# A SwiGLU block behind linear attention on one core: the first product of the last down projection is split by a second Strassen level too

## The chip, the core and the metric

The kernel runs on one core of a Trainium2 chip. TensorE (PE) multiplies matrices and writes to PSUM, VectorE (DVE) and ScalarE (ACT) take results out of PSUM and do elementwise work, GpSimd (POOL) does elementwise work between SBUF operands and issues some DMAs, and SyncE (SP) issues most DMAs. The metric is the device time of one execution in microseconds (us); the kernel before takes 757.95 us (median of three runs, 757.32 to 758.75).

## The reference

```python
xn = layernorm(x)                        # x: 2048 x 1024
s  = linear_attention(xn, wqkv) @ wo     # 32 heads of 32
g  = silu((silu(xn @ w_gate) * (xn @ w_up)) @ w_down)   # 1024 -> 3584 -> 1024
out = x + s * g
```

All inputs and the output are bf16. What the change touches is the last product, `(...) @ w_down`, for one half of the 2048 rows.

## The kernel before

The feed-forward part works in two passes of 1024 rows. In a pass, `h` holds the product of gate and up, transposed: `h[:, c, :]` is row chunk `c` (128 of the 3584 hidden columns) by 1024 tokens. The pass has 28 *units*, 14 pairs of a gate unit and an up unit, each for 256 hidden columns. A unit is one matrix product by Strassen (Winograd's form): `emit_a` issues four products of four matmuls of 512 columns, `emit_b` three more. They interleave on PE: the `a` part of unit i+1 stands ahead of the `b` part of unit i. So the `a` part of unit k starts when the `b` part of unit k-2 is done. `emit_c22` and `emit_evac` take a unit's results out of PSUM with ACT and DVE. `x_` and `y_` are PSUM banks of pool `pps` (4 banks), `zw` pairs of banks of pool `ppd` (2 pairs).

A unit's weights and their four Strassen sums were packed in DRAM earlier (`pk_g`, `pk_u`) and come back in one DMA of 1 MB into a slot of the ring `wgu` (8 slots, `w_slot`). `load_w_to(n)` issues the loads up to the n-th in the sequence `w_seq`; a load whose slot is still in use waits at the head of SP's queue, and everything behind it on SP waits too.

After the units of the last pass, `emit_down_m` computes the down projection of that pass by Strassen: seven products M1 to M7 over quadrants of `h` (A11, A12, A21, A22) and of `w_down`, in the order 1, 2, 7, 6, 5, 4, 3. A plain product is 56 matmuls of 512 columns (4 row tiles by 14 chunks, line L1400). M2 and M4 are split once more (`L2 = (2, 4)`, function `l2_M`): each becomes seven products of 14 matmuls of 256 columns (L1433), with partial results copied between PSUM banks by ACT (L1449, L1455) and added by DVE (L1388). `KA` and `KB` are fp32 buffers in SBUF that hold M1 and the running sums of M1, M7 and M6.

The second level needs sums of quadrants on both sides:

- Of the weights, *staging* does it during the units of the last pass. `l2_load` takes a ring slot and issues the loads of two of the seven chunk pairs (four DMAs of 128 KB, L1109; two for the last pair), `l2_sums` does four subtractions on POOL (L1122) and stores the seven blocks to DRAM with a DMA from POOL (L1123, 896 KB). There are four such steps for a product, so eight for M2 and M4, one in every third unit (`i % 3`).
- Of `h`, `l2_lhs` does four sums on POOL per chunk pair (L1139 to L1142), into two `kept` tiles that the first pass left over (`x_spare`). For M2 it runs during the units, for the last chunk pair and for M4 afterwards.

At the end `fin` multiplies by `s` (L1176), adds `x` (L1177) and stores (L1178).

Of the kernel before, what the change touches and what calls it, by code (L numbers as in the profile page):

```python
# [21 lines left out]
def kernel(  # L22
# [168 lines left out]
    L2 = (2, 4)  # L191
    L2_ORDER = (1, 5, 2, 6, 7, 4, 3)
# [759 lines left out]
    with ExitStack() as p3:  # L952
# [4 lines left out]
        p3a = ExitStack()  # L957
        pps = p3a.enter_context(tc.tile_pool(name="p3ps", bufs=4, space=PSUM, reuse_waits="tile"))
        ppd = p3a.enter_context(tc.tile_pool(name="p3pd", bufs=2, space=PSUM, reuse_waits="tile"))
# [62 lines left out]
        def emit_evac(key, h, tail=None):  # L1022
            p, kind, fg = key
            x_, zw, s2, s3, _, *c = grp.pop(key)
            rc = rc_of(key)
            if kind == "g":
                cf = m4.tile([P, 2, TB], FP32, name="cg", tag="m4")
                d12 = cf[:]
            else:
                c = c[0]  # L1030
                d12 = c[:, 0:2, :]
                sg = sg_tiles.pop((p, fg))
                nc.vector.scalar_tensor_tensor(out=h[:, 2 * fg, 0:TB], in0=x_[:], scalar=rc, in1=sg[:, 0, :],
                                               op0=ALU.mult, op1=ALU.mult)
            nc.vector.scalar_tensor_tensor(out=d12, in0=zw[:], scalar=rc,  # L1035
                                           in1=s2[:, None, :].to_broadcast([P, 2, TB]), op0=ALU.mult, op1=ALU.add)
            if kind == "g":
                sg = m4.tile([P, 4, TB], BF16, name="sg", tag="m4")
                sg_tiles[(p, fg)] = sg
                nc.scalar.activation(out=sg[:, 3, :], in_=s3[:], func=ACT.Silu)  # L1040
                nc.scalar.activation(out=sg[:, 0, :], in_=x_[:], func=ACT.Silu, scale=rc)
                nc.scalar.activation(out=sg[:, 1:3, :], in_=cf[:], func=ACT.Silu)  # L1042
            else:
                if tail is not None:
                    tail()
                hv = h[:, 2 * fg:2 * fg + 2, :].rearrange("p a b -> p (a b)")
                nc.vector.tensor_tensor(out=hv[:, TB:4 * TB], in0=c[:].rearrange("p a b -> p (a b)"),
                                        in1=sg[:, 1:4, :].rearrange("p a b -> p (a b)"), op=ALU.mult)
# [51 lines left out]
        def l2_load():  # L1100
# [5 lines left out]
            for j in js:  # L1106
                for k, b0, b1 in ((0, 0, 7), (1, 2, 6)):
# [4 lines left out]
        def l2_sums():  # L1112
# [5 lines left out]
            def b(i):  # L1118
                r = v[:, i, 0:n_, :]
                return r.bitcast(F16) if i in (1, 3, 4, 5) or M >= 4 else r  # L1120
            for o_, a_, b_ in ((1, 7, 0), (3, 6, 1), (4, 6, 7), (5, 2, 3)):
                nc.gpsimd.tensor_tensor(out=b(o_), in0=b(a_), in1=b(b_), op=ALU.subtract)  # L1122
            nc.gpsimd.dma_start(out=l2_drams[M][:, :, js.start:js.stop, :], in_=v[:, 0:7, 0:n_, :])  # L1123

        x_spare = []

        def l2_bufs():
            v = [x[:].rearrange("p a b -> p (a b)").bitcast(F16)[:, 0:2 * NQ * 2 * P].rearrange(
                "p (s j r n) -> p s j r n", s=2, j=NQ, r=2) for x in x_spare]
# [6 lines left out]
        def l2_lhs(A, j, eng):  # L1136
            a11, a12, a21, a22 = l2_quad(A, j)
            s1, s2, s3, s4 = [v[:, j] for v in l2_bufs()]
# [226 lines left out]
        def emit_down_m(p, h, base):  # L1365
# [8 lines left out]
            def load(M, q=None):  # L1374

                load_w_to(base + max(i for i, key in enumerate(seq) if key[2][0] == M and q in (None, key[2][1])) + 1 + NPK)
# [30 lines left out]
            p3a.close()  # L1407
            ppm = p3.enter_context(tc.tile_pool(name="p3m8", bufs=2 * TPB, space=PSUM, reuse_waits="tile"))

            def banks(n=TPB):  # L1410
                return [ppm.tile([P, CW], FP32, name="dm", tag="m")[:] for _ in range(n)]
# [10 lines left out]
            def l2_p(M, i, r, A, bk):  # L1422
# [6 lines left out]
                for j in range(NQ):  # L1429
                    q = l2_quad(A, j)  # L1430
                    sb = [v[:, j] for v in l2_bufs()]
# [4 lines left out]
            def l2_M(M, A, K, done, fill, in_place):  # L1436
# [3 lines left out]

                def xw(r):
                    return bk[2 * r]

                def zy(r):
                    return bk[2 * r + 1]
                for i, r in ((1, 0), (5, 0), (1, 1), (5, 1)):
                    l2_p(M, i, r, A, bk)
                for r in range(2):
                    nc.scalar.copy(out=zy(r)[:, hi], in_=xw(r)[:, lo])  # L1449
                load(M, 0)  # L1450
                c = [[k2([P, CW], FP32, "l2c")[:] for _ in range(2)] for r in range(2)]
                for r in range(2):
                    l2_p(M, 2, r, A, bk)
                    l2_p(M, 6, r, A, bk)
                    nc.scalar.copy(out=zy(r)[:, lo], in_=zy(r)[:, hi])  # L1455
                    tt(K[2 * r][:, hi] if in_place else c[r][0][:, hi], zy(r)[:, hi], K[2 * r][:, hi])
                load(M, 1)
                for r in range(2):
                    l2_p(M, 7, r, A, bk)
                for r in range(2):  # L1460
                    tt(c[r][1][:, hi], zy(r)[:, lo], K[2 * r + 1][:, hi])
                    tt(c[r][1][:, hi], xw(r)[:, hi], c[r][1][:, hi])
                    if not in_place:
                        tt(c[r][0][:, lo], xw(r)[:, lo], K[2 * r][:, lo])
# [4 lines left out]
                for r in range(2):  # L1469
                    tt(c[r][1][:, lo], zy(r)[:, lo], K[2 * r + 1][:, lo])  # L1470
                    done(2 * r + 1, c[r][1])
                    l2_p(M, 3, r, A, bk)
                    if in_place:
                        tt(c[r][0], xw(r), K[2 * r])
                    else:
                        tt(c[r][0][:, hi], xw(r)[:, hi], c[r][0][:, hi])
                    done(2 * r, c[r][0])
                load(M, 3)

# [7 lines left out]
            load_w_to(base + NPK)  # L1487
            bk = banks()
            E = [bk[2], bk[3], bk[0], bk[1]]
            KA = kept("kA")  # L1490
            for t0 in (0, 2):
                for k in range(NFG):
                    for t in (t0, t0 + 1):
                        mm(1, t, k, E[t], True)
                for t in (t0, t0 + 1):
                    nc.scalar.copy(out=KA[t], in_=E[t])
            load(1)
            for k in range(NFG):
                tt(S3(k), A11[:, k], A21[:, k], ALU.subtract)
            sums(S1, A21, A22, ALU.add)  # L1500

# [10 lines left out]
            l2_M(2, quads(h, 1, 0), KA, done2, fill7, False)  # L1512
# [8 lines left out]
            for j in range(NQ):  # L1521
                l2_lhs(quads(h, 1, 1), j, nc.gpsimd)
# [29 lines left out]
            l2_M(4, quads(h, 1, 1), KB, done4, fill3, True)  # L1552
# [18 lines left out]
        for pi, p in enumerate(passes):  # L1571
# [71 lines left out]
            l2_steps = [] if first else list(l2_q)  # L1643
# [6 lines left out]
            for i in range(n):  # L1650
                if first:
                    load_w_to(base + i + (na0 if i < n - 7 else 8 if i > n - 6 else 7))
                else:
                    load_w_to(base + i + (6 if i < 3 * len(l2_steps) else 8))
# [34 lines left out]
                if not first:  # L1689
                    if i % 3 == 0 and l2_q:  # L1690
                        l2_load()
                    if i % 3 == 1 and l2_live:
                        l2_sums()
                    if i % 4 == 0 and i >= 4:
                        l2_lhs(quads(h, 1, 0), i // 4 - 1, nc.gpsimd)
                    if i == n - 1:
                        l2_lhs(quads(h, 1, 0), NQ - 1, nc.gpsimd)
# [3 lines left out]
            if last_pass:  # L1701
                emit_down_m(p, h, base)
# [35 lines left out]
```

## Time and profile before

| What | Value |
|---|---|
| median of the runs | 757.95 us |
| profiled execution, its own time | 757.71 us |
| span of its trace | 755.9 us |
| PE busy | 746.6 us, 99% |
| DVE, ACT, POOL busy | 573.5, 379.5, 361.1 us |
| TensorE clock granted | 1.00 |
| DMA, mean over the span | 242 GB/s |
| last pass: first `a` part to the last `b` part | 497.66 to 667.36 us |
| down projection of the last pass on PE | 667.36 to 751.31 us |

Busy time tells little of PE here: matmuls overlap, so a group's busy time is longer than its share of the span, and the distance between the starts of two groups is the better measure. The chain of waits is read from its end: each piece is what the next one waited for. In the timelines of SP and POOL a DMA's row is its issue, not its transfer.

### The profile page before, as it was taken

What the parts mean: (1) busy time and instruction counts of PE and PEld (TensorE: products, weight loads), DVE (VectorE), ACT (ScalarE), POOL (GpSimd) and SP (SyncE); (2) the same over time, 40 slices, a digit from 0 to 9 for tenths busy, and PEclk for the clock granted to TensorE, in tenths of its full rate; (3) what the DMA queues carried; (4) which work ended last, traced back from release to release, by engine and by line L of the source; (5) the groups of instructions that cost most, each with busy time, mean ns of one, the idle gap of its engine ahead of it and who ended that gap; (6) DMA issues with size and microseconds to landing.
All of it is one profiled execution on the core that took longest, in us unless ns stands there. A gap on an engine that the chain in (4) does not pass through costs nothing.

```text
span 755.9 us, 10887 instructions
## 1 busy us (share of the span) xinstructions
PE 746.6 (99%) x3815; PEld 356.8 (47%) x3815; DVE 573.5 (76%) x1036; ACT 379.5 (50%) x537; POOL 361.1 (48%) x444
## 2 busy tenths in 40 slices
PE   8999999999999999999999999999999999999997
PEld 3544444454544444444444444444444444446464
DVE  6687787886796788888889765369686777784965
ACT  5677776898956565666659301142322223212023
POOL 2444799999540276858675000115344433113900
PEclk9999999999999999999999999999999999999999
DMA  9967799979779667878899236498867567748452
GB/s 318 304 146 137 234 329 301 306 157 270 217 180 304 232 215 280 315 275 308 279 331 391 92 120 242 131 373 296 307 248 275 194 241 251 266 156 257 165 169 82
DMA packets 123896, 183.19 MB, mean 242 GB/s; under 512 B 35936, under 2 KB 99424, under 8 KB 114112
## 3 DMA queue, kind: packets, MB, share of 16 engines
q1 hardware_dynamic: 116496, 151.41, 62.3%
q0 software_dynamic: 5904, 28.58, 9.9%
q10 hardware_dynamic: 1440, 2.49, 1.0%
q8 instruction: 30, 0.49, 0.3%
q14 instruction: 26, 0.21, 0.1%
HBM read 118.10 MB, written 57.02 MB: 232 GB/s over the span
## 4 chain that ended last, share of the span: by engine, by line
PE 96%; DVE 2%; issue 1%; DMA 0%; ACT 0%; DVEq 0%; ACTq 0%
PE zw L966 25%; PE kv_ps L554 15%; PE xb L966 12%; PE q_ps L183 7%; PE dm L1400 7%; PE dzw L1204 6%; PE yb L966 6%; PE dx L1204 3%; PE s_ps L774 3%; PE fx L816 3%; PE dm L1433 3%; PE dy L1204 2%; PE nd L743 1%; PE kvz L576 1%; DVE g L1176 1%
## 5 line engine op out<-in xcount | busy, mean ns | idle before, releaser
L966 PEld LDWEIGHTS <-w_sb 128*128 128x128 f16 (+1 forms) x1568 | 152.2, 98 | 183.2 <-issue 0.6
L966 PE MATMUL xb<-xnT,w_sb 128*128 128x512 bf16 x448 | 115.0, 379 | 0.0
L554 PE MATMUL kv_ps<-wkv_sb,xnT 128*128 128x512 bf16 x512 | 113.7, 379 | 0.6 <-ACT xnT L543 0.4
L966 PE MATMUL zw<-S,w_sb 128*128 128x512 f16 x448 | 105.8, 379 | 0.3 <-DVE cu L1035 0.3
L966 PE MATMUL zw<-xnT,w_sb 128*128 128x512 bf16 x448 | 105.8, 379 | 0.0
L321 POOL TENSOR_TENSOR w_sb<-w_sb 128x512 f16<-128x512 bf16 x42 | 50.7, 1207 | 93.4 <-DVE w_sb L309 51.3
L286 ACT ACTIVATE w_sb<-w_sb 128x2048 bf16<-128x2048 bf16 x42 | 79.9, 1902 | 4.3 <-DMA w_sb<-in_B_w_up_dram 3.2
L554 PEld LDWEIGHTS <-xnT 128*128 128x128 bf16 x512 | 48.3, 98 | 55.9 <-ACT xnT L543 0.8
L1122 POOL TENSOR_TENSOR w_sb<-w_sb 128x512 f16<-128x512 bf16 (+3 forms) x32 | 34.6, 1103 | 61.0 <-DMA w_sb<-wd 52.3
L1042 ACT ACTIVATE sg<-cg 128x1024 bf16<-128x1024 f32 x28 | 29.6, 1057 | 57.4 <-DVE cg L1035 57.4
L183 PE MATMUL q_ps<-xnT,wq_sb 128*128 128x512 bf16 x256 | 58.4, 379 | 0.0
L966 PE MATMUL yb<-S,w_sb 128*128 128x512 f16 x224 | 57.4, 378 | 0.0
L1035 DVE SCALAR_TENSOR_TENSOR cg<-zw,rc_all,s 128x1024 f32<-128x1024 f32 x28 | 35.9, 1283 | 25.1 <-PE zw L966 13.2
L322 POOL TENSOR_TENSOR w_sb<-w_sb 128x512 f16<-128x512 bf16 x42 | 50.8, 1209 | 3.3
L1178 POOL DMA_DIRECT2D out_dram<-io x16 | 8.9, 566 | 90.8 <-DVE io L1177 90.6
L994 DVE SCALAR_TENSOR_TENSOR s<-yb,rc_all,s 128x512 f32<-128x512 f32 x42 | 31.4, 748 | 27.0 <-ACT s L993 27.0
L324 POOL TENSOR_TENSOR w_sb<-w_sb 128x512 f16<-128x512 bf16 x42 | 50.7, 1208 | 0.0
L1400 PE MATMUL dm<-w_sb,hT 128*128 128x512 f16 (+3 forms) x238 | 49.2, 366 | 1.2 <-DVE cu L1035 1.2
L323 POOL TENSOR_TENSOR w_sb<-w_sb 128x512 f16<-128x512 bf16 x42 | 50.3, 1198 | 0.0
L1204 PE MATMUL dx<-w_sb,hT 128*128 128x512 bf16 x112 | 42.4, 379 | 0.0
L993 ACT ACTIVATE s<-xb,rcl 128x512 f32<-128x512 f32 x14 | 9.6, 688 | 65.3 <-PE xb L966 65.3
L993 ACT ACTIVATE s<-xb,rc_all 128x512 f32<-128x512 f32 x42 | 28.4, 676 | 21.9 <-issue 12.9
(203 smaller groups left out, 1286.5 us busy)
## 6 DMA issues: line engine op xcount, KB each, us to landing
w_sb<-pk_g SPq DMA_DIRECT2D x27, 1024.0 KB, 6.8
pk_g<-w_sb SPq DMA_DIRECT2D x14, 1024.0 KB, 5.3
w_sb<-pk_u SPq DMA_DIRECT2D x14, 1024.0 KB, 6.7
pk_u<-w_sb POOLq DMA_DIRECT2D x13, 1024.0 KB, 5.4
w_sb<-wd SPq DMA_DIRECT2D x30, 256.0 KB, 4.3
w_sb<-in_B_w_gate_dram SPq DMA_DIRECT2D x14, 512.0 KB, 6.3
w_sb<-in_B_w_down_dram SPq DMA_DIRECT2D x28, 256.0 KB, 5.0
w_sb<-in_B_w_up_dram SPq DMA_DIRECT2D x14, 512.0 KB, 5.5
```

Source lines behind the costliest of these rows:

```text
L183: nc.tensor.matmul(q_ps[:], lhsT=wq_sb[:, dc, g * P:(g + 1) * P], rhs=xn_ap(dc, btok), start=(dc == 0), stop=(dc == DC - 1))
L286: nc.scalar.activation(out=junk, in_=raw_view(key, t), func=ACT.Square, accum_out=asum[:])
L321: nc.gpsimd.tensor_tensor(out=T1, in0=b12, in1=b11, op=ALU.subtract)
L322: nc.gpsimd.tensor_tensor(out=T2, in0=b22, in1=T1, op=ALU.subtract)
L323: nc.gpsimd.tensor_tensor(out=T3, in0=b22, in1=b12, op=ALU.subtract)
L324: nc.gpsimd.tensor_tensor(out=T4, in0=b21, in1=T2, op=ALU.subtract)
L554: mm = nc.tensor.matmul(kv_ps[:], lhsT=xn_ap(dc, tok), rhs=wkv_sb[:, dc, c * CW:(c + 1) * CW], start=(dc == 0), stop=(dc == DC - 1))
L966: mm = nc.tensor.matmul(out, lhsT=lhs(k), rhs=rhs(k), start=(first and k == 0), stop=(k == HK - 1), skip_group_check=True)
L993: nc.scalar.activation(out=s1[:], in_=x_[:], func=ACT.Copy, scale=rc)
L1035: nc.vector.scalar_tensor_tensor(out=d12, in0=zw[:], scalar=rc, in1=s2[:, None, :].to_broadcast([P, 2, TB]), op0=ALU.mult, op1=ALU.add)
L1204: nc.tensor.matmul(out, lhsT=lhs, rhs=rhs, start=first, stop=lastk, skip_group_check=True)
L1400: nc.tensor.matmul(out, lhsT=lhs_of(M)(k)[:, t * P:(t + 1) * P], rhs=w_of(M, k)[:, cols], start=first and k == 0, stop=k == NFG - 1, skip_ ...
```

## The change

M1 goes through `l2_M` as well. Its results are needed in SBUF as they are (`KA`), so for `K is None` ACT copies them there.

- The staging has twelve steps (three products), one in each of the units 3 to 14; `l2_sums` of a step comes one unit later. The loads of the weights run up to five units ahead in units 0 to 16 and six ahead after that, instead of six and eight.
- The sums of A11 need room: from unit 15 on two slots of the ring are taken for them (`r_spare`) until M1 is done. `l2_lhs` for M1 and M2 runs from unit 17 on, one chunk pair of both in a unit; the last pair of M1 comes right after its part of `h` is written, in `emit_evac`.
- `l2_M` becomes a generator. Its order is P1, P1, P2, P2, then P5, P6, P5, P6 and so on (it was P1, P5, P1, P5, P2, P6, P2, P6), and it yields after P2. M1 calls `next(m2)` as its filler, so P1 and P2 of M2 run between P7 and P4 of M1.
- The sums S3 on DVE come ahead of M1 in the program, the sums S1 after it.
- The PSUM pool `pps` stays open for the down projection and gives every second set of four banks; the other sets come from a new pool in the place of `ppd`.

```diff
-    L2 = (2, 4)
-    L2_ORDER = (1, 5, 2, 6, 7, 4, 3)
+    L2 = (1, 2, 4)
+    L2_ORDER = (1, 2, 5, 6, 7, 4, 3)
...
+                if p == passes[-1] and fg == NFG - 1:
+                    l2_lhs(1, quads(h, 0, 0), NQ - 1, nc.gpsimd)
                 hv = h[:, 2 * fg:2 * fg + 2, :].rearrange("p a b -> p (a b)")
...
-            p3a.close()
-            ppm = p3.enter_context(tc.tile_pool(name="p3m8", bufs=2 * TPB, space=PSUM, reuse_waits="tile"))
+            p3d.close()
+            ppm = p3.enter_context(tc.tile_pool(name="p3m4", bufs=TPB, space=PSUM, reuse_waits="tile"))
+            turn = [0]
 
             def banks(n=TPB):
-                return [ppm.tile([P, CW], FP32, name="dm", tag="m")[:] for _ in range(n)]
+                turn[0] += 1
+                pool, tg = (pps, "s") if turn[0] % 2 else (ppm, "m")
+                return [pool.tile([P, CW], FP32, name="dm", tag=tg)[:] for _ in range(n)]
...
-                for i, r in ((1, 0), (5, 0), (1, 1), (5, 1)):
-                    l2_p(M, i, r, A, bk)
+                xw, zy = bk[0::2], bk[1::2]
                 for r in range(2):
-                    nc.scalar.copy(out=zy(r)[:, hi], in_=xw(r)[:, lo])
-                load(M, 0)
-                c = [[k2([P, CW], FP32, "l2c")[:] for _ in range(2)] for r in range(2)]
+                    l2_p(M, 1, r, A, bk)
+                for r in range(2):
+                    nc.scalar.copy(out=zy[r][:, hi], in_=xw[r][:, lo])
                 for r in range(2):
                     l2_p(M, 2, r, A, bk)
+                load(M, 0)
+                yield
+                for r in range(2):
+                    l2_p(M, 5, r, A, bk)
                     l2_p(M, 6, r, A, bk)
-                    nc.scalar.copy(out=zy(r)[:, lo], in_=zy(r)[:, hi])
-                    tt(K[2 * r][:, hi] if in_place else c[r][0][:, hi], zy(r)[:, hi], K[2 * r][:, hi])
+                    nc.scalar.copy(out=zy[r][:, lo], in_=zy[r][:, hi])
                 load(M, 1)
                 for r in range(2):
                     l2_p(M, 7, r, A, bk)
...
+                    if K is None:
+                        nc.scalar.copy(out=c1[:, hi], in_=zy[r][:, lo])
+                        nc.scalar.copy(out=c0[:, hi], in_=zy[r][:, hi])
+                        nc.scalar.copy(out=c0[:, lo], in_=xw[r][:, lo])
+                    else:
+                        tt(c1[:, hi], zy[r][:, lo], K[2 * r + 1][:, hi])
+                        tt(K[2 * r][:, hi] if in_place else c0[:, hi], zy[r][:, hi], K[2 * r][:, hi])
...
-            load_w_to(base + NPK)
-            bk = banks()
-            E = [bk[2], bk[3], bk[0], bk[1]]
+            load_w_to(base + NPK - 2)
             KA = kept("kA")
-            for t0 in (0, 2):
-                for k in range(NFG):
-                    for t in (t0, t0 + 1):
-                        mm(1, t, k, E[t], True)
-                for t in (t0, t0 + 1):
-                    nc.scalar.copy(out=KA[t], in_=E[t])
-            load(1)
-            for k in range(NFG):
-                tt(S3(k), A11[:, k], A21[:, k], ALU.subtract)
-            sums(S1, A21, A22, ALU.add)
...
-            l2_M(2, quads(h, 1, 0), KA, done2, fill7, False)
+            m2 = l2_M(2, quads(h, 1, 0), KA, done2, fill7, False)
+            for k in range(NFG):
+                tt(S3(k), A11[:, k], A21[:, k], ALU.subtract)
+            go(l2_M(1, quads(h, 0, 0), None, None, lambda: next(m2), False, KA))
+            sums(S1, A21, A22, ALU.add)
+            go(m2)
...
-                    load_w_to(base + i + (6 if i < 3 * len(l2_steps) else 8))
+                    load_w_to(base + i + (5 if i < 5 + l2_n else 6))
...
-                    if i % 3 == 0 and l2_q:
+                    if l2_live:
+                        l2_sums()
+                    if i in (3 + l2_n, 4 + l2_n):
+                        r_spare.append(w_slot())
+                    if i >= 3 and l2_q:
                         l2_load()
-                    if i % 3 == 1 and l2_live:
-                        l2_sums()
-                    if i % 4 == 0 and i >= 4:
-                        l2_lhs(quads(h, 1, 0), i // 4 - 1, nc.gpsimd)
-                    if i == n - 1:
-                        l2_lhs(quads(h, 1, 0), NQ - 1, nc.gpsimd)
+                    if i > 4 + l2_n and 4 * l2_j + 4 <= i:
+                        l2_lhs(1, quads(h, 0, 0), l2_j, nc.gpsimd)
+                        l2_lhs(2, quads(h, 1, 0), l2_j, nc.gpsimd)
+                        l2_j += 1
...
             if last_pass:
+                l2_lhs(2, quads(h, 1, 0), NQ - 1, nc.gpsimd)
                 emit_down_m(p, h, base)
```

## The prediction

> **What bounds the kernel now.** First the page's busy shares, for the engine that counts; then the chain of waits around the end of the units and the down projection, for the gaps of that engine; then the timeline of PE, for the pitch of its matmuls; last the timelines of SP and POOL in the units, for the staging.
>
> ```profile
> PE 746.6 (99%) x3815; PEld 356.8 (47%) x3815; DVE 573.5 (76%) x1036; ACT 379.5 (50%) x537; POOL 361.1 (48%) x444
> ```
>
> PE is the bound. The chain from 655 to 700 us (start, us, what) shows what its other 1% looks like here:
>
> ```profile
> 665.80 1.74 PE zw L966 x8
> 667.54 0.03 issue
> 667.57 1.29 DVE cu L1035
> 668.86 0.04 issue
> 668.90 12.03 PE dm L1400 x55
> 680.93 6.13 PE dm L1433 x56
> 687.06 0.02 issue
> 687.08 0.37 ACT dm L1455
> 687.45 0.02 issue
> 687.47 0.44 DVE l2c L1388
> 687.95 0.92 PE dm L1433 x7
> ```
>
> The units end, M1 waits for DVE to empty the last `zw`, and M2 waits for a copy and an add ahead of its second P7.
>
> ```profile
> 688.71 3.18 PE L1400 MATMUL dm<-w_sb,S3h 128*128 128x512 f16 x14
> 691.73 1.69 PE L1433 MATMUL dm<-w_sb,hT 128*128 128x256 f16 x14
> 693.26 1.69 PE L1433 MATMUL dm<-w_sb,kept 128*128 128x256 bf16 x14
> 694.79 9.23 PE L1400 MATMUL dm<-w_sb,S3h 128*128 128x512 f16 x42
> ```
>
> In PE's timeline the starts give the pitch: 14 matmuls of 512 columns in 691.73-688.71 = 3.02 us, 0.216 us each; 14 of 256 columns in 693.26-691.73 = 1.53 us, 0.1094 each.
>
> One staging step, first on SP (the loads, and the weight load that waits for the slot), then on POOL (the sums and the store):
>
> ```profile
> 541.02 2.19 SPq L1109 DMA_DIRECT2D w_sb<-wd  x4
> ...
> 556.86 0.33 SPq L263 DMA_DIRECT2D w_sb<-pk_u  x1
> ```
>
> ```profile
> 547.20 4.62 POOL L1122 TENSOR_TENSOR w_sb<-w_sb 128x512 f16<-128x512 bf16 x4 [12.33 <-DMA w_sb<-wd]
> 552.12 0.91 POOL L1123 DMA_DIRECT2D l<-w_sb  x1 [0.30 <-POOL w_sb L1122]
> ...
> 597.34 5.33 POOL L1122 TENSOR_TENSOR w_sb<-w_sb 128x512 f16<-128x512 f16 x4 [10.21 <-DMA w_sb<-wd]
> ```
>
> The step holds its slot from 541.02 to 556.86, 15.84 us: 6.18 until the data are there, 4.62 for the sums, 0.30, and 4.74 from the store's issue until the slot is free. The other full steps held theirs 17.76 (573.20 to 590.96), 16.32 (591.38 to 607.70) and 17.82 us (608.87 to 626.69).
>
> The landing times of single DMAs, first of the staging loads (L1109), then of the 1 MB weight loads (L263, from 490 us on), and one stretch early in the pass with the time of each engine, the granted clock, the DMA share and GB/s at its end:
>
> ```profile
> DMA to landing us min/median/max: 3.1/5.1/7.1
> ```
>
> ```profile
> DMA to landing us min/median/max: 4.8/7.4/16.2
> ```
>
> ```profile
> 505.50:511.60 6.10, 6.10 (x30) 2.77 (x29) 4.33 (x7) 2.32 (x3) 0.54 (x1) 1.00 1.02 428
> ```
>
> So some 400 GB/s is what the DMA engines give, and a staging load needs 5 to 8 us with other loads ahead of it.
>
> **The change, part by part, against the profiled execution's own 757.71 us** (0.24 under the median of 757.95).
>
> *M1's matmuls.* Out: 56 of 0.216 us, 12.10 us. In: 7 x 14 = 98 of 0.1094 us, 10.72 us. All of it is on PE's path: -1.38. A page speaks against this term. The Trainium skill, "TensorE: Matmul & The Clock Gate", section "Back-to-back issue gap", gives a sustained spacing of 131 ns for 512 columns and 81 ns for 128; between them an estimate for 256 is 98 ns, and by that M1 would go from 7.3 to 9.6 us, a loss of 2.3, and the sum below would come to 758.5. The rows say 216 and 109 ns, so halving the columns halves the time here, and I go by them.
>
> *The start of M1.* From 667.36, its first matmul, to 668.90 there are 1.54 us for one matmul of 0.216: 1.32 idle. The first banks now come from `pps`; their last reader is the up unit's DVE operation on `xb` (L1033), 666.18 to 666.92, ahead of 667.36. The pair that `cu` empties until 668.86 is first written by M2, some 7.7 us later. -1.32; the bounds are that and 0, should the new banks be free no earlier; the row of L1033 is the nearest. New there: P2 waits for ACT's copy of P1. P1 of the other row half (0.77) covers that copy (0.36).
>
> *The wait inside M2 and M4.* From 667.36 to 694.79 PE has 12.10+10.72+3.02 = 25.84 us of matmuls in 27.43: less the 1.32, 0.27 are M2's wait at 687. M4: 728.03 to 742.05 is 14.02 for 13.74, 0.28. The add moves behind P7, and the copy alone (0.36) lies beside the other half's P7 (0.77). -0.55; bounds 0 and -0.55, taken whole since the add that ended the wait is out of its way.
>
> *The early stall.* At 527.51 PE waited 0.33 for `cu`, late behind final multiplies on DVE that ran 1.37 and 1.26 us instead of 0.42 while POOL did sums of the first step. No sums run at that time now. -0.33 (bounds 0 and -0.33).
>
> *Costed at nothing, with the cover.* The 28 more sums of `h` on POOL, 0.72 each: 8 in a unit from unit 17 on, done near 640, needed at 670. The last pair's four for M1 start at 666.9 and end near 670; P5 wants the first at 670.4, P3 the last at 679.7. Eight copies of 0.36 on ACT, idle from 667.4. S1 on DVE (4.3 us) now after M1, 681.7 to 686.0; M2's adds queue behind it and its P4 needs the first at 688.8, since M7's first tile (3.02) lies between: 2.4 to spare. S2 then ends 1.2 ahead of M6, as before (702.67 against 703.86). On SP, M2's first quarters wait for the slots of units 26 and 27 (665.0, 667.4) and land 6.9 later (row of these loads), at 672 and 674; P1 of M2 starts at 675.0, P5 at 681.2. M7's second half waits for M2's P2 (678.1): four issues and 4.3 to land, 685, needed at 687.3. Beyond these margins of 2 to 3 us each us late costs one.
>
> *The staging.* Here a stall may come. In the changed kernel's instruction order six slots go round among the weights and two among the steps; I call the step of unit n tn. t5 waits for the store of t3, t7 for t5's, t9, t11, t13 likewise; the weights of units 12, 14, 16 and 18 wait for the stores of t6, t8, t10 and t12, those of 20 for t13's; t8, t10, t12 follow those weights on SP. All stand in one queue. On POOL, t3's sums stand behind the last deferred output store, which DVE releases at 521.5: start 522.4, store 527.4, free 532.1; unit 9's weights share the transfer, so 533.5 for t5. A link of the odd chain has no 1 MB load ahead in the queue, unlike every row of before: load 4.9 (the fourth issue starts 1.5 after the first, and lands 3.1 to 3.5 later, the low end of the landing times), sums 4.8 (rows 4.62 and 5.33), 0.3, store 4.74, and 0.5 for the even step's store beside it: 15.2. t13 goes out at 533.5+4x15.2 = 594.3. t11 went at 579.1 and its sums keep POOL until 590.0; t12's sums 590.0 to 594.8, its store 595.1, free 599.8: then unit 18's weights, which land 4.8 to 7.4 us later (fastest and median row), 604.6 to 607.2. Unit 18 wants them when unit 16 ends: 531.82+12x6.045 = 604.4. Late by 0.2 to 2.8; I take 0.7, near the fast end, because t13's data are in by 599 and nothing is ahead. Unit 20's come at 609.5+(4.8 to 7.4) = 614.3 to 616.9, wanted at 616.5+0.7: no more. +0.7; bounds 0 (before had no such wait to lose) and 13 (all links of 17.82, unit 20 with 7.4).
> The Trainium skill, "SBUF — State Buffer", section "SBUF: two separate sides", has DVE and GpSimd lock their shared ports for a whole instruction; a step whose sums lost one L1047 (0.96 us) would take 5.6 instead of 4.8, and by that unit 18 would be some 4 late and the sum 758. Two of the six full rows show such a loss, 5.33 for 4.62, so I keep the mixed 4.8.
>
> Sum: -1.38-1.32-0.55-0.33+0.70 = -2.88, 754.8 in the profile's terms; with the 0.24, **755.1**.
>
> **The rivals.** *The staging chain stalls PE (slower).* The rows of before hold a slot 15.84 to 17.82 us, mean 16.9. With links of that, t13 goes at 533.5+4x16.9 = 601.1, its slot is free at 618.0, unit 20's weights land at 625.4 with the median 7.4, 8.9 late: -3.58+8.9 = +5.3, **763.3**. For it: a full step and a weight load are 1.05+0.52+0.92 = 2.49 MB, in every unit of 6.045 us 412 GB/s, all that the DMA engines gave in the stretch above; a store that shares them takes longer than 4.74. Against: those rows had one or two 1 MB loads ahead, and the chain slows itself to two steps and two weight loads a link, at most 328 GB/s over 15.2 us. It decides above 16.1 us a link (5.1 late, the gain and 0.2%).
>
> *The end gains nothing but the matmuls.* If `pps` is no earlier free than `ppd`, or M1's own copies make waits like M2's 0.27, then -1.38+0.27+0.70 = -0.4: **757.5**. For: every split product so far has that wait. Against: the row of L1033, and the order of the copies.
>
> **How the numbers follow.** 0.2% is 1.5 us, about what a measurement tells from no change. Likeliest (0.64): no stall above 2 us, 754.0 to 756.4. The chain's rival 0.25: late by 2 to 5 within 0.2% (0.06), more is slower (0.19). The end's rival 0.11: 0.09 within, 0.02 faster. Faster 0.66, same 0.15, slower 0.19. The range 754.0 to 761.0 leaves out about 0.06 below (all bounds at once and no stall) and 0.1 above, links near 16.5 and up.
>
> **What would show it.** M1's first matmul straight after the units and no DVE `cu` before it in the chain; 196 matmuls of 256 columns between the units and M7, M7's second tile some 24.5 us after the units instead of 27.4; no ACT or DVE piece between P6 and P7. In the units: slots held 14 to 16 us by the odd steps, and at most one gap of PE near 604, waiting for a DMA of `w_sb`. I am wrong if PE waits for weights at units 16 to 21 for more than 2 us, if the gap moves to M2's first weights near 675, or if DVE ends S2 after M6 wants it.

## The result, and the profile after

The changed kernel takes 765.83 us (median of four runs, 763.14 to 768.63) against 758.07 beside it: a ratio of 1.0103, 95% interval 1.0065 to 1.0141. It is slower by 1%, where 755.1 and faster was predicted, and outside the range up to 761.0. The profiled execution took 766.05 us, its span is 764.2, 8.3 longer than before's 755.9. All positions below are from the profiled executions.

PE's line of the page, and the three waits of PE that the changed kernel has from the units on (us in total, times, longest):

```profile
PE 748.9 (98%) x3857; PEld 361.9 (47%) x3857; DVE 576.3 (75%) x1040; ACT 381.4 (50%) x545; POOL 400.9 (52%) x492
```

```profile
PE yb L966 <- DMA w_sb<-pk_g: 7.1, 2, 4.5
...
PE dm L1441 <- ACT dm L1453: 0.3, 1, 0.3
```

PE waited twice for a gate unit's 1 MB of weights, 7.1 us in all; before it never did. PE's timeline has the two places, with the groups after each:

```profile
595.82 1.04 PE L966 MATMUL yb<-S,w_sb 128*128 128x512 f16 x4 [2.66 <-DMA w_sb<-pk_g]
596.69 1.03 PE L966 MATMUL xb<-xnT,w_sb 128*128 128x512 bf16 x4
597.56 1.89 PE L966 MATMUL zw<-S,w_sb 128*128 128x512 f16 x8
...
612.56 1.89 PE L966 MATMUL yb<-S,w_sb 128*128 128x512 f16 x4 [4.48 <-DMA w_sb<-pk_g]
614.24 1.91 PE L966 MATMUL xb<-xnT,w_sb 128*128 128x512 bf16 x4
615.95 2.82 PE L966 MATMUL zw<-S,w_sb 128*128 128x512 f16 x8
```

Read the starts, not the durations. After the first wait the groups follow 0.87 us apart, as everywhere. After the second they follow 1.68 and 1.71 apart: half speed. The granted clock in two windows of one unit each (it is the third number from the end of a row, then the DMA share and GB/s) agrees:

```profile
608.90:614.95 6.05, 2.39 (x6) 0.89 (x7) 0.50 (x1) 1.06 (x1) 4.89 (x5) 0.67 0.95 367
614.95:621.00 6.05, 6.05 (x23) 2.45 (x22) 2.91 (x4) 0.69 (x1) 4.47 (x7) 0.76 0.58 181
```

A unit puts 28 matmuls of 0.216 us on PE, so the `yb` groups, one to a unit, should start 6.045 us apart. They start at 586.95, 595.82, 601.87, 612.56 and 621.19: excesses of 2.83, 0, 4.64 and 2.59, in sum 10.06. The last one, 2.59, holds no wait; it is the half clock alone.

The end of the last pass, from the chain of waits (start, us, what):

```profile
676.61 1.73 PE zw L966 x8
678.34 18.34 PE dm L1441 x168
696.68 3.02 PE dm L1405 x14
699.70 3.06 PE dm L1441 x28
702.76 33.25 PE dm L1405 x154
...
736.76 0.72 ACT g L1427
737.48 0.28 ACT dm L1453
737.80 6.28 PE dm L1441 x56
```

Nothing stands between the units and M1 any more, and 196 matmuls of 256 columns run without a piece of ACT or DVE between them (18.34 for 168 is 0.109 each). In PE's timeline M1's first matmul and M7's second tile are these:

```profile
678.17 3.22 PE L1441 MATMUL dm<-w_sb,hT 128*128 128x256 bf16 x28
...
702.59 9.23 PE L1405 MATMUL dm<-w_sb,S3h 128*128 128x512 f16 x42
```

From the one to the other it is 24.42 us, where before it was 27.43 (667.36 to 694.79): -3.01. The budget of the 8.3 us, by PE's timeline:

| Where | us |
|---|---|
| up to unit 16 (586.95 against 586.21) | +0.74 |
| waits of units 16 and 18 (2.83 + 4.64) | +7.47 |
| half clock after the second | +2.59 |
| M1 and M2, from their start to M7's second tile | -3.01 |
| from there to the end (61.61 against 61.11) | +0.50 |

So the end gave what it was to give, and the staging took it back three times over. The first row does not come from the staging: the first unit of the first pass, ahead of all that was changed in the units, already starts 1.23 later (244.57 against 243.34), and from unit 0 to unit 16 of the last pass the changed kernel is 0.49 faster (88.06 against 88.55). The runs below that have no wait ahead of unit 16 start it at 586.35 to 586.84.

What PE waited for, from the chain ahead of the second wait:

```profile
590.32 6.73 DMA w_sb<-wd
...
598.45 3.40 POOL w_sb L1124 x3
...
602.13 5.40 DMA l<-w_sb
...
607.59 4.92 DMA w_sb<-pk_g
...
612.56 1.89 PE yb L966 x4
```

A staging step's load, its sums, its store, then the weights that wanted the step's slot: the chain of the prediction's first rival. SP's timeline gives the issues of the odd steps' loads, the weights of unit 18, and the weights of unit 20, which mark when t13's slot was free:

```profile
537.89 1.94 SPq L1111 DMA_DIRECT2D w_sb<-wd  x4
...
553.02 1.92 SPq L1111 DMA_DIRECT2D w_sb<-wd  x4
...
569.19 1.94 SPq L1111 DMA_DIRECT2D w_sb<-wd  x4
...
585.97 2.51 SPq L1111 DMA_DIRECT2D w_sb<-wd  x4
...
602.22 2.26 SPq L1111 DMA_DIRECT2D w_sb<-wd  x4
607.59 0.33 SPq L263 DMA_DIRECT2D w_sb<-pk_g  x1
...
619.30 0.33 SPq L263 DMA_DIRECT2D w_sb<-pk_g  x1
```

The links are 15.13, 16.17, 16.78, 16.25 and 17.08 us, mean 16.3. POOL's timeline splits them; t3's store, and t9 as an example:

```profile
528.53 0.93 POOL L1125 DMA_DIRECT2D l<-w_sb  x1 [0.30 <-POOL w_sb L1124]
...
575.40 5.21 POOL L1124 TENSOR_TENSOR w_sb<-w_sb 128x512 f16<-128x512 bf16 x4 [5.25 <-DMA w_sb<-wd]
580.91 0.90 POOL L1125 DMA_DIRECT2D l<-w_sb  x1 [0.30 <-POOL w_sb L1124]
```

t9: 569.19 to 575.40 until its data are in, 5.21 of sums, 0.30, and 580.91 to 585.97 until the slot is free. Over the five links the means are 5.20 (load), 4.81 (sums), 0.30, and 5.98 (store until free).

### The profile page after: what moved, and what is told of

It reads as the page before. It is cut to its first block, busy times and chain, and to the rows that moved or that the text cites. A ratio compares the mean times of both kernels' runs of the same rounds, so it can differ in the third digit from the quotient of the medians.

```text
span 764.2 us, 11064 instructions
## 1 busy us (share of the span) xinstructions
PE 748.9 (98%) x3857; PEld 361.9 (47%) x3857; DVE 576.3 (75%) x1040; ACT 381.4 (50%) x545; POOL 400.9 (52%) x492
## 3 DMA queue, kind: packets, MB, share of 16 engines
q10 hardware_dynamic: 1440, 2.49, 0.9%
## 4 chain that ended last, share of the span: by engine, by line
PE 73%; issue 11%; DMA 7%; POOL 3%; DVE 3%; ACT 1%; SPq 1%; POOLq 0%; DVEq 0%; ACTq 0%
PE zw L966 18%; PE kv_ps L554 15%; PE xb L966 9%; PE q_ps L183 6%; PE dm L1405 6%; PE yb L966 4%; DMA l<-w_sb 4%; PE dm L1441 4%; PE fx L816 3%; PE s_ps L774 2%; DMA w_sb<-wd 2%; POOL w_sb L1124 2%; PE dzw L1208 1%; POOL out_dram L1182 1%; PE kvz L576 1%
## 5 line engine op out<-in xcount | busy, mean ns | idle before, releaser
L1124 POOL TENSOR_TENSOR w_sb<-w_sb 128x512 f16<-128x512 bf16 (+3 forms) x48 | 50.3, 1071 | 31.5 <-DMA w_sb<-wd 30.6
L309 DVE TENSOR_SCALAR w_sb<-w_sb,cs_all 128x2048 bf16<-128x2048 bf16 x35 | 36.4, 1039 | 2.8
```

## Experiments

Two theories of the waits had to be told apart. The *chain theory* (A in the expectations): the slot is held too long, and it is the sum of load, sums and store that counts. The *engine theory* (C): the DMA engines are full, 2.49 MB in every unit of 6.045 us, and the chain is only where it shows. A third, B in the first expectations, is that the added bytes and sums cost time wherever they lie. Beside them stood the question of what the end really gained, and what made the half clock.

### Does the end gain what was said?

The changed kernel without the staging of M1; M1's second level reads the blocks that M2's staging made, so all matmuls are there.

```diff
-        l2_q = deque((M, j) for M in L2 for j in range(0, NQ, 2))
+        l2_q = deque((M, j) for M in L2 if M != 1 for j in range(0, NQ, 2))
...
-                nc.sync.dma_start(out=l2_slot(t)[:, 0:n_], in_=l2_drams[M][:, 2 * hf:2 * hf + n_])
+                nc.sync.dma_start(out=l2_slot(t)[:, 0:n_], in_=l2_drams[max(M, 2)][:, 2 * hf:2 * hf + n_])
```

> The change without the four staging steps of M1; M1 multiplies by the prepared blocks of M2 instead, so M1 is wrong. Eight steps remain, one in each of the units 3 to 10. Theory A: the chain of slots ends before its lag has used up the lead; the last weights that hang on it are those of units 16 and 17, and PE waits at most 1 us: 755 to 756.5 us. Theory B: two thirds of the staging at the same density, two thirds of the waits, 4 us or more and a lowered clock: 760 or more.

755.38 us (755.10 to 755.54) against 758.16: 0.9963, interval 0.9948 to 0.9977. PE has no wait in the units, and from M1's start to M7's second tile it takes the same 24.42 us. That is what A expected and not B. The end's gain is there, 2.8 us, and the whole loss comes with the third product's staging.

The part of it that the prediction put on the start of M1 can be had alone: the kernel before with only the change's PSUM pools.

```diff
-        p3a = ExitStack()
-        pps = p3a.enter_context(tc.tile_pool(name="p3ps", bufs=4, space=PSUM, reuse_waits="tile"))
-        ppd = p3a.enter_context(tc.tile_pool(name="p3pd", bufs=2, space=PSUM, reuse_waits="tile"))
+        p3d = ExitStack()
+        pps = p3.enter_context(tc.tile_pool(name="p3ps", bufs=4, space=PSUM, reuse_waits="tile"))
+        ppd = p3d.enter_context(tc.tile_pool(name="p3pd", bufs=2, space=PSUM, reuse_waits="tile"))
...
-            ppm = p3.enter_context(tc.tile_pool(name="p3m8", bufs=2 * TPB, space=PSUM, reuse_waits="tile"))
+            ppm = p3.enter_context(tc.tile_pool(name="p3m4", bufs=TPB, space=PSUM, reuse_waits="tile"))
...
-                return [ppm.tile([P, CW], FP32, name="dm", tag="m")[:] for _ in range(n)]
+                turn[0] += 1
+                pool, tg = (pps, "s") if turn[0] % 2 else (ppm, "m")
+                return [pool.tile([P, CW], FP32, name="dm", tag=tg)[:] for _ in range(n)]
```

> The kernel before, with nothing but the changed kernel's PSUM pools: the four banks of the units stay allotted into the last pass and the products take turns between two sets of four banks; M1 stays plain. The prediction put 1.3 us of its gain on the start of M1, which in the kernel before waits for banks still being emptied. If that gain comes from the pools alone, about 756.8 (758.1 less 1.3), with no idle time of the matmul engine ahead of M1; if it comes with the order of the new M1 (its products over 2 banks first), 758.1 and the same wait. The weights and the units are those of before, so no theory of the staging expects a change here.

756.91 us (11 runs, 756.51 to 758.32) against 758.08: 0.9984, interval 0.9976 to 0.9993. Its chain goes from the units straight into a plain M1, with no `cu` between:

```profile
666.33 1.73 PE zw L966 x8
668.06 12.09 PE dm L1400 x56
```

From M1's first matmul to M2's first it is 12.09 us (667.89 to 679.98 in PE's timeline) instead of 13.41 (667.36 to 680.77): the 1.32 of the prediction, from the pools alone. The whole run gained 1.2.

### What made the half clock?

Twelve and twenty matmuls that nothing needs were put ahead of units 16 and 18, where PE had been idle; they write a bank that the unit then overwrites.

```diff
+            for _ in range({(0, "g", 8): 12, (0, "g", 9): 20}.get(key, 0)):
+                nc.tensor.matmul(y_[:], lhsT=x1[:, 0, 0:P], rhs=x1[:, 1, :], start=True, stop=True,
+                                 skip_group_check=True)
             prod(y_[:], lambda k: T2[:, k, :], lambda k: S2[:, k, :], True)
```

> The change with matmuls that nothing needs put ahead of unit 16 (12) and unit 18 (20), 0.216 us each, 2.6 and 4.3 us, where PE waited 2.66 and 4.48 us. If the half-speed matmuls after the second wait come from the idle time (the granted clock fell to 0.67 there), they are gone and the time is 2 to 3 us under the change's, near 763. If they come from something else at that time (weights still landing, ports), they stay, and the time is that of the change, 766.

762.51 us (762.29 to 763.65), 1.006, interval 1.0047 to 1.0073; some 3.3 under the changed kernel, though the weights come no earlier. PE's timeline at unit 18:

```profile
612.75 1.04 PE L966 MATMUL yb<-S,w_sb 128*128 128x512 f16 x4 [0.23 <-DMA w_sb<-pk_g]
613.62 1.03 PE L966 MATMUL xb<-xnT,w_sb 128*128 128x512 bf16 x4
```

The unit starts when it did (612.56 before), and its groups follow 0.87 apart. So the slow matmuls came of PE's standing still, and not of anything else that happened at that time.

### Chain or engines?

First the steps were spread, two in three units from 3 to 19, the two slots for the sums of A11 taken at units 21 and 22.

```diff
-                    load_w_to(base + i + (5 if i < 5 + l2_n else 6))
+                    load_w_to(base + i + (5 if i < 23 else 6))
...
-                    if i in (3 + l2_n, 4 + l2_n):
+                    if i in (21, 22):
                         r_spare.append(w_slot())
-                    if i >= 3 and l2_q:
+                    if i >= 3 and i % 3 != 2 and l2_q:
                         l2_load()
```

> The change with its twelve staging steps spread over units 3 to 19, two in three units instead of one in each; the two slots for the sums of A11 are taken in units 21 and 22, and these sums run in units 23 to 26. Same work, same bytes. Theory A (the slots of the staging steps turn over more slowly than one step a unit, some 8.1 us a step against 6.05, and the weight loads queue behind them): two steps in 18.1 us is slower than two links of 16.3 take, so PE waits for no weights, never drops its clock, and the gain at the end is left: 755 us (754.5 to 756). Theory B (the extra 6.4 MB and 19 us of POOL work hurt wherever they lie): waits for weights of some microseconds remain, 760 or more.

761.66 us (758.41 to 763.12), 1.0039, interval 1.0024 to 1.0054: better than the change and worse than before. A had expected 755 and no wait; B's 760 or more came, but the run with a step in every second unit, below, moves the same bytes and does the same sums without a wait, so B does not hold as it stands. Two waits are left, later ones:

```profile
626.22 1.89 PE L966 MATMUL yb<-S,w_sb 128*128 128x512 f16 x4 [3.16 <-DMA w_sb<-pk_u]
...
647.24 1.04 PE L966 MATMUL yb<-S,w_sb 128*128 128x512 f16 x4 [1.39 <-DMA w_sb<-pk_g]
```

SP's timeline shows why spreading bought so little:

```profile
555.51 0.33 SPq L263 DMA_DIRECT2D w_sb<-pk_g  x1
555.90 0.43 SPq L263 DMA_DIRECT2D w_sb<-pk_u  x1
563.96 1.91 SPq L1111 DMA_DIRECT2D w_sb<-wd  x4
```

Two weight loads now went out back to back, beside a store of 448 KB (the short last step of a product) issued at 555.29, and that store's slot was free only at 563.96: 8.67 us. The next store, 896 KB at 572.35, had no such company and took 4.75. A link's length depends on what shares the engines with it.

Then the chain was shortened in time but loaded in bytes: the sums left out, and two more DMAs of 256 KB in each full step.

```diff
+                src = wd_drams[j][0 if kd == "a" else 1][:, 0:2, q].rearrange("p k (c n) -> p k c n", n=CH)
+                nc.sync.dma_start(out=v[:, 2:6, j - j0, :].rearrange("p (k c) n -> p k c n", k=2), in_=src)
...
-            for o_, a_, b_ in ((2, 7, 0), (3, 6, 2), (4, 6, 7), (5, 1, 3)):
-                nc.gpsimd.tensor_tensor(out=b(o_), in0=b(a_), in1=b(b_), op=ALU.subtract)
```

> The change with the four sums of each staging step left out; the four blocks are filled by two more DMAs of 256 KB from the same tensors, so the prepared weights are wrong. The slot is held some 3 to 4 us less (no 4.6 to 5.2 us of sums, 0.9 to 1.5 us more of issues), while 6 MB more are moved. Theory A: links of 12.5 to 13.5 us, no waits for weights, 754.5 to 756. Theory C (the DMA engines are the limit in units 3 to 14): more bytes in the same stretch, longer waits than in the change, 768 or more.

773.57 us (767.99 to 775.17), 1.019, interval 1.0163 to 1.0217. Without the sums the waits are twice as long, 14.3 us. In two of these three windows the engines are full:

```profile
530.00:545.00 15.00, 15.00 (x72) 6.77 (x70) 10.52 (x13) 4.22 (x6) 0.90 (x1) 1.00 1.02 348
545.00:560.00 15.00, 15.00 (x71) 6.84 (x70) 9.90 (x12) 5.17 (x7) 1.78 (x2) 1.00 0.73 246
560.00:575.00 15.00, 14.56 (x69) 6.40 (x67) 11.45 (x15) 3.54 (x5) 1.78 (x2) 1.00 1.04 352
```

A share of 1.0 moved 350 GB/s here, not the 428 that the prediction had read off a stretch of mostly 1 MB weight loads. At that point the engine theory looked right for the change as well. The next run took the sums out and left the bytes as the change has them; the store writes one raw block seven times.

```diff
-            for o_, a_, b_ in ((2, 7, 0), (3, 6, 2), (4, 6, 7), (5, 1, 3)):
-                nc.gpsimd.tensor_tensor(out=b(o_), in0=b(a_), in1=b(b_), op=ALU.subtract)
-            nc.gpsimd.dma_start(out=l2_drams[M][:, :, js.start:js.stop, :], in_=v[:, 0:7, 0:n_, :])
+            nc.gpsimd.dma_start(out=l2_drams[M][:, :, js.start:js.stop, :], in_=v[:, 0:1, 0:n_, :].to_broadcast([P, 7, n_, CH]))
```

> The changed kernel without the four subtractions of each staging step; the store writes one raw block seven times, so the same bytes go over the same queues behind the same waits, and only GpSimd's 4.6 to 5.2 us a step are gone (the three products of the last pass that use the blocks get wrong weights, their matmuls are all there). Theory A (latency of the chain load, sums, store, next load): a link of 16.3 becomes about 11.4, far under 16.1: no wait of the matmul engine in the units, 754.5 to 756. Theory C (DMA engines full): each unit still moves 2.49 MB, 7.3 us at 340 GB/s against 6.05: the chain gives its time back to longer stores and loads, waits of 2 us and more remain around units 16 to 20, 760 or more.

758.12 us median of ten; the ratio is 1.0007, interval 0.9982 to 1.0032, without the longest of them; but five of the ten took 755.9 to 757.2 and the others 759.1 to 767.8. The profile is of one at 756.29, and only 0.2 us of waiting is left in it:

```profile
530.00:545.00 15.00, 15.00 (x71) 6.77 (x70) 10.52 (x13) 4.22 (x6) 1.79 (x2) 1.00 0.97 338
545.00:560.00 15.00, 15.00 (x71) 6.81 (x70) 9.90 (x12) 5.17 (x7) 1.78 (x2) 1.00 0.94 326
560.00:575.00 15.00, 15.00 (x71) 6.79 (x70) 11.45 (x15) 3.54 (x5) 2.54 (x3) 1.00 0.98 346
575.00:590.00 15.00, 15.00 (x71) 6.84 (x70) 11.34 (x13) 4.74 (x7) 1.69 (x3) 1.00 0.77 252
```

Up to 575 the engines carried the change's bytes at a share of 0.94 to 0.98. With the sums in the chain, in the changed kernel, the first three windows have 0.85, 0.88 and 0.74, and 284, 299 and 258 GB/s; the last of them:

```profile
560.00:575.00 15.00, 15.00 (x71) 6.80 (x70) 11.83 (x14) 3.64 (x5) 8.28 (x8) 1.00 0.74 258
```

There the engines are not full, they wait for the chain. That is against the engine theory as the cause of the change's loss, and for the chain theory, but not without a remainder. The four links from t5's to t13's load took 11.65, 14.53, 22.05 and 12.02 without the sums, mean 15.06, where 11.4 was expected and the changed kernel has 16.08: most of what the sums gave up, the transfers and their order took. In the third, t11's load waited for the store of t10, issued at 574.25, and not for that of t9. t13's load goes out at 591.18 instead of 602.22, and 7.0 of these 11.0 us were gained at the head, where t5's goes out at 530.93 instead of 537.89. The other half of the runs has no trace; that they waited for a transfer, with the engines so nearly full, is likely and not shown.

Last, fewer bytes with the chain's parts all there: each step stores only its four sums (512 KB for 896), and the unchanged blocks are read in the last pass from where the weights lie.

```diff
-                nc.sync.dma_start(out=l2_slot(t)[:, 0:n_], in_=l2_drams[M][:, 2 * hf:2 * hf + n_])
+                if hf in (1, 2):
+                    nc.sync.dma_start(out=l2_slot(t)[:, 0:2], in_=l2_drams[M][:, 2 * hf - 2:2 * hf])
+                else:
+                    for j in range(NQ):
+                        src = wd_drams[j][0 if kd == "a" else 1]
+                        if hf:
+                            nc.sync.dma_start(out=l2_slot(t)[:, 0, j], in_=src[:, 1, q, CH:CW])
+                        else:
+                            nc.sync.dma_start(out=l2_slot(t)[:, 0:2, j], in_=src[:, 0:2, q, 0:CH])
...
-            nc.gpsimd.dma_start(out=l2_drams[M][:, :, js.start:js.stop, :], in_=v[:, 0:7, 0:n_, :])
+            nc.gpsimd.dma_start(out=l2_drams[M][:, :, js.start:js.stop, :], in_=v[:, 2:6, 0:n_, :])
```

> The changed kernel, but each staging step writes only the four blocks that were computed (512 KB instead of 896 KB); the three unchanged blocks of a product are read straight from where the weights lie, in seven smaller transfers each, during the last pass. Theory A (a slot of the ring is held too long, link by link): a link loses the store's share, 3/7 of some 4.7 us = 2.0, so 16.3 becomes 14.3, under the 16.1 from which the units wait: no wait in units 16 and 18, about 755. Theory C (the DMA engines are full in units 3 to 14, giving some 340 GB/s on this mix): 2.49 MB a unit become 2.10 MB, 6.2 us at 340 GB/s against a unit of 6.05, so a backlog of some 2 us over 12 units instead of 15: small waits or none, 755 to 757, above all no idle time over 3 us and so no half clock. Neither tells the other off here; what the run tells is whether the bytes of the staging alone bring the time from 765.8 to below 758.1. If the time stays at 760 or more, both are wrong on the price of the store.

761.35 us (760.05 to 761.75), 1.0041, interval 1.0027 to 1.0055. Both theories missed: waits of 1.50, 1.89 and 1.13 us stayed, with a DMA share of 0.69 to 0.75 from 545 to 590 us. The engines had room, and the chain was late all the same. From its issue to the next odd load a store took 3.97 us on average, 2.0 less as expected, but the loads took 6.56 instead of 5.20, and four links (t5's to t13's load) average 15.96 against 16.08. SP's timeline shows what the loads met:

```profile
545.93 0.33 SPq L271 DMA_DIRECT2D w_sb<-pk_u  x1
546.32 3.22 SPq L1119 DMA_DIRECT2D w_sb<-wd  x4
...
561.84 0.33 SPq L271 DMA_DIRECT2D w_sb<-pk_u  x1
562.22 2.19 SPq L1119 DMA_DIRECT2D w_sb<-wd  x4
```

From t7 on every odd load came directly behind 1 MB of weights; in the changed kernel t7's, t9's and t11's went ahead of theirs (553.02 against 555.11 for t7's). What SP waited for from 536 to 612 us says why. In the changed kernel the five odd loads wait for a store themselves, 46.3 us in all, beside three waits of weights. Here no staging load does: eleven waits, 60.2 us, are all of weights, which take the slots that the stores free, and the loads stand behind them. The run without the sums is like that too (nine waits of weights, one of a staging load). So in neither is the sums' time or the store's bytes the only thing that differs from the changed kernel. What the run gained, it gained at the head of the chain: t3's store took 3.9 us instead of 9.36, and t5 went out at 531.80 instead of 537.89.

### A version that beats both

If the chain decides, it wants time, not bytes: one step in every second unit (0 to 22), so that a link has four units, 24.2 us. The two slots for the sums of A11 come at units 23 and 24, those sums in units 25 to 27.

```diff
-                    load_w_to(base + i + (5 if i < 5 + l2_n else 6))
+                    load_w_to(base + i + (5 if i < 2 * l2_n + 1 else 6))
...
-                    if i in (3 + l2_n, 4 + l2_n):
+                    if i in (2 * l2_n - 1, 2 * l2_n):
                         r_spare.append(w_slot())
-                    if i >= 3 and l2_q:
+                    if i % 2 == 0 and l2_q:
                         l2_load()
-                    if i > 4 + l2_n and 4 * l2_j + 4 <= i:
-                        l2_lhs(1, quads(h, 0, 0), l2_j, nc.gpsimd)
-                        l2_lhs(2, quads(h, 1, 0), l2_j, nc.gpsimd)
-                        l2_j += 1
+                    if i % 4 == 0 and i >= 4:
+                        l2_lhs(2, quads(h, 1, 0), i // 4 - 1, nc.gpsimd)
+                    for j in {25: (0, 1, 2), 26: (3, 4), 27: (5,)}.get(i, ()):
+                        l2_lhs(1, quads(h, 0, 0), j, nc.gpsimd)
```

> The changed kernel with one staging step in every second unit (units 0 to 22) in place of every unit from 3 to 14; the two ring slots for the sums of A11 are taken at units 23 and 24 and the sums made in units 25 to 27. Theory A (the chain of one slot: load, sums, store, next load): steps two apart now have four units, 24.2 us, for a link that took 14.5 to 17.1 us, so no wait of the matmul engine in the units; with the end's gain as the run without M1's staging had it, about 755.4. Theory C (DMA engines full): 1.77 MB a unit at 340 GB/s are 5.2 us against 6.05, so no wait either, 755.4. Both then rest on the density of the steps. Third possibility: the two slots taken late cost on their own, as the waits of units 21 and 24 in the run with two steps in three units did; then waits of 1 to 3 us around units 23 to 27 and 757 to 761.

756.32 us (7 runs, 755.87 to 757.13) against 758.34: 0.9971, interval 0.9960 to 0.9982. No wait in the units; in the last pass PE waits for these two:

```profile
PE dm L1441 <- ACT dm L1453: 0.3, 1, 0.3
PE dm L1441 <- POOL w_sb L1143: 0.2, 1, 0.2
```

With the small store as well:

> As the kernel with a step in every second unit, and each step stores only the four computed blocks (the unchanged blocks are read where the weights lie, during the last pass). With the link's budget at 24.2 us the smaller store is worth nothing to theory A or C: 755.4, no wait. If the kernel with every second unit still waits around units 23 to 27, the smaller store shortens that by some 2 us a link; if the small reads of the last pass cost, the last pass is longer than the 24.4 us from M1's start to the second tile of M7.

756.01 us (6 runs, 755.60 to 756.16), 0.9966, interval 0.9954 to 0.9978: the same within what can be told, as both theories had it. From M1's first matmul to M7's second tile both take 24.81 us, 0.39 more than the changed kernel; as it is the same in both, it is not the small reads. Neither run tells the chain theory from the engine theory, since both expected no wait. Both do the whole computation, and both are faster than the kernel before by 2.0 and 2.3 us. So the idea of the change holds; its calendar did not.

## Why the prediction was wrong

*M1's matmuls, -1.38; the start of M1, -1.32; M2's wait, -0.27.* Right: -2.97 expected up to M7's second tile, -3.01 measured, 1.32 of them shown alone by the pools. 256 columns took 0.109 us each, as the rows of before said.

*M4's wait, -0.28.* Wrong in a small way. The add that ended it is gone, but ACT's copy now stands behind ACT's silu (736.76 to 737.48 in the chain), and PE waits the same 0.3. From M7's second tile to the end of M4 it is 47.40 us instead of 47.26. Another 0.36 of the +0.50 lies behind PE's last matmul; no run isolates it.

*The early stall, -0.33.* The wait is gone, and by the starts it was worth 0.49 (unit 0 to unit 16, above). That the change took it away is not shown: the run with the pools alone stages as the kernel before does, and in its trace the wait is gone too, with the same 88.06 us (498.68 to 586.74).

*The staging, +0.70: the step that failed*, with +10.06 measured, 7.47 of waits and 2.59 of half clock. Its picture was right: the odd chain, the weights behind it on SP, the place. Its sizes were not:

| Term | Predicted | Measured |
|---|---|---|
| t3's store issued, to t5's load | 6.1 | 9.36 |
| a load, until the sums start | 4.9 | 5.20 |
| sums | 4.8 | 4.81 |
| store until the slot is free | 5.24 | 5.98 |
| a link (of t5, t7, t9, t11, t13) | 15.2 | 16.3 |
| t13's load goes out | 594.3 | 602.22 |
| t12's store issued | 595.1 | 602.13 |
| unit 18's weights land | 604.6 to 607.2 | 612.51 |

Of the 7.9 us by which t13 is late, 4.4 come from the head (3.3 of them t3's store, 1.1 its later start) and 3.5 from four links that are 0.9 longer. Unit 18 hangs on t12, whose sums follow t11 on POOL: t11's load went out 6.9 late (585.97 for 579.1), and t12's store 7.0 late. The sums, the only part that has no transfer in it, were right to 0.01. The loads of t5 and t7 took 3.9 and 3.7 us; those of t9 and t13, issued within 0.1 us of the even step's full store, took 6.2 and 7.5. Each transfer had been priced near the fast end of the rows, and a chain adds such errors up: 0.3 in the load and 0.7 in the store of every link, and 3.3 in the first store, decided the sign. The bound was there to be read: the full stores of the kernel before landed 4.7 to 9.4 us after their issue.

*The rival.* "The staging chain stalls PE" put its deciding link at 16.1 us; 16.3 came. It expected 8.9 us of waiting at unit 20, and 7.47 came at units 16 and 18. Unit 16's wait was not priced: its weights take t10's slot, free at 588.7, and stand behind t11's load in SP's queue, which waited for t9's slot until 585.97; they went out at 588.96 and took 6.8 us. The argument against this rival, that the chain slows itself to what the engines can carry, is true of the bytes (0.74 to 0.88 of the share) and says nothing about whether PE waits. For it, the prediction named 412 GB/s of demand against 400 of supply; supply is some 345 with these loads in the mix, but with a share of 0.74 to 0.88 from 530 to 590 us the changed kernel did not reach it; the runs without the sums and with the small store point to it as the next limit.

*The half clock, in no case of the prediction*: +2.6 to 3.3, and the reason why the time lies above even the rival's 763.3 with a chain that was better than the rival's.

*The skill's rules.* The estimate from the sustained spacing of the Trainium skill's "TensorE: Matmul & The Clock Gate", section "Back-to-back issue gap", would have made M1 longer; the rows and the run without M1's staging say it is shorter. The estimate that went with the shared ports of "SBUF — State Buffer", section "SBUF: two separate sides", would have made a step's sums 5.6 us; they took 4.59 to 5.21, mean 4.81.

## What to carry to other kernels

A chain of load, compute, store and reload through one buffer slot must be priced with the slow rows of its transfers, because they meet each other; compare the sum of a link with the pace of the consumer. Here two units are 12.09 us, so that already the planned link of 15.2 fell 3.1 behind each time and lived on the ring's lead; at 16.3, after a late head, the lead was used up at unit 16. Then give the chain time before you take bytes from it: here a step in every second unit instead of every unit turned a loss of 7.8 us into a gain of 2.0, and 16% fewer bytes did not. Look at the head of such a chain apart from its links; a late start is carried through all of it, and most of what the runs without the sums and with the small store gained on t13's load was gained there. A wait of PE of some 3 us or more is not paid with its own length alone: 1.3 to 2.6 us of half clock came after it here.

## What the runs showed that was not expected

- *Idle time and the clock.* After waits of PE of 0.2 to 1.9 us (nine of them in the units, over the experiments) and of 2.66 us the next groups ran at full speed; after 3.16, 3.17, 4.48, 4.74 and 5.30 they ran at half, until a unit's excess of 1.3 to 2.6 us had built up. The Trainium skill, "TensorE: Matmul & The Clock Gate", section "What's actually happening", has the clock fall to a half after about 3.4 us of idling, in windows that run on their own. The runs put the bound between 2.66 and 3.16 us of waiting, a little under that; the unequal cost after nearly equal waits fits windows that are not tied to the wait.
- *The DMA engines' rate depends on what they carry.* A share of 1.0 was 428 GB/s in a stretch of mostly 1 MB weight loads and 348 to 352 GB/s with staging loads and stores among them.
- *A store's time depends on company.* In the changed kernel an 896 KB store took from 4.7 us to 9.36 us until its slot was free. One of 448 KB took 8.67 us beside two 1 MB loads issued right after it; in the kernel before the two of that size landed after 3.6.
